# Set attention and gated feed-forward on one core: eight buffers for hi and lo, rows of x and transposed x in one ring

## Chip, cores and metric

One core of one Trainium2 chip runs the whole program. The metric is the device time in microseconds, the median of three runs; lower is better.

## What is computed

Input x has 4 batches of 12480 tokens with 128 channels. Each batch goes through two attentions with 32 inducing points, and every token of the result through a feed-forward layer with 2048 hidden units:

```python
h = mab(I, x)          # softmax(scale * I x^T) x: 32 rows per batch
a = mab(x, h)          # softmax(scale * x h^T) h: 12480 rows per batch
g = a @ w_in
g = g * (1 / (1 + exp(-1.702 * g)))
out = g @ w_out
```

The softmax of the first attention runs over all 12480 tokens of a batch, so the batch has to be read once for `h`, and a second time for the second attention.

## The kernel before, in words

**The feed-forward loop.** Tokens are worked in 98 items, 96 of 512 tokens and 2 of 384 (what is left over of two batches each). Each item has 8 steps, so there are 784 steps; a step is 256 of the 2048 hidden units. In a step PE makes two matrix products into a PSUM tile `ph` (L542, `firsts`). ACT turns `ph` into `g` with the gate function (L568). `g` is then split into a rounded part `hi`, by ACT straight from `ph` (L584) or by DVE from `g` (L591), and a rest `lo` = g - hi, by DVE (L600). Then PE makes six products into `pso`, three for each of two 128-row chunks: hi with the low part of the weights (L729), lo with the high part (L730), hi with the high part (L731). This is `seconds`. After 8 steps `pso` is copied out (L620 on ACT, L623 on DVE) and stored. The first 12 steps use whole weights instead (L715) and no hi and lo.

**The rings.** `ph` has 2 buffers, `g` 3, `hi` 6 and `lo` 6 (constant `HELD`). The tiles of hi and lo lie in a pool `ph_`; each has a gap of 16 elements behind it (`spaced`, `STEP`).

**The order of the work.** Nothing is scheduled on the chip: while the program is built, a planner (`Plan`) holds a list of threads, each a generator of jobs with an engine, an assumed duration, the buffers that they read, write and take, a rank and sometimes a gate. At each step it emits the job that can start first (start time plus its own delay, then rank). The order in which jobs are emitted is the fixed order of each engine's instructions, and of the DMAs in the queue of SP.

What steers it is the **lead**, `ahead()`: steps whose lo has been emitted (`counts["L"]`), less steps whose six products have been emitted (`counts["S"]/2`). `counts["F"]` is the number of steps whose first products have been emitted. The constants `AHEAD` = 4 and `LUMP` = 5 enter in four places:

- `late` (L507): first products are held back by 800 ns while the lead is at least `AHEAD`, and visits of the attention (groups of PE work, below) may then begin with a longer delay.
- `tarry` and `filler` (L510 to L514): attention work on ACT and DVE gets a delay of 400 ns and a low rank while the lead is below `AHEAD`.
- `by_then` (L516): the same, but only until `counts["F"]` has reached a due step.
- the exponentials (L907 and L1080): they need another table of ACT than the gate function, so they are put together in lumps of three or four sets. A lump may go when the lead is at least `LUMP`, or when `counts["F"]` has reached a last step.

**The attention of batches 1 to 3** runs beside the feed-forward loop, one batch ahead. For batch b (`attention`, L818): PE makes the first scores from transposed x (`first_into`, L352) in two or three visits; they are copied out and their maximum is taken; ACT makes two lumps of exponentials (L900); DVE transposes them; PE sums the rows of x with these weights in three visits (`weigh`, L371; `WEIGH` is [0, 1], [2, 3], [4, 5, 6]); a chain on DVE makes h; then `second` (L1032) makes the scores of the second attention from transposed x again (`second_into`, L360) in two visits, and two more lumps of exponentials (L1074). `lay_out` (L1110) normalizes them, splits them, and sends them by DMA into the tiles `st` that the first products read.

**The loads.** A batch is cut into seven sets: six of 2048 tokens and one of 192. Transposed x is loaded twice per batch, in 1 MB loads into the ring `r_xt` of 4 buffers (`loads_xT`, L744 to L761): all sets for the first scores, then all for the second. Rows of x are loaded once, in four DMAs of 256 KB for each set (`loads_x`, L763 to L777), into the ring `r_xn` of 2 buffers in the pool `pn`, which is opened when the last weights are decoded (`finish`, L1359); the loads wait for `counts["F"]` at 40 steps behind the batch's first (`loads_x` is spawned at L837). The two lists of loads are two threads of the planner; all go through the queue of SP.

Of the kernel before, what the change touches and what calls it, by code (L numbers as in the profile page):

```python
# [8 lines left out]
F32 = mybir.dt.float32  # L9
I32 = mybir.dt.int32  # L10
F32R = mybir.dt.float32r
# [6 lines left out]
P = 128  # L18
TOP = -(1 << 30)
TOK = 512  # L20
BLK = TOK // 32
RG = 2
HELD = 6
AHEAD = 4
LUMP = 5
LEAD = 24
SLACK = 3000.0
WC = 512
# [1 line left out]
XB = 4  # L30
# [66 lines left out]
class Ring:  # L97
# [8 lines left out]
    def free(self, ahead):  # L106
        k = len(self.units) + ahead - self.bufs
        if k < 0:
            return 0.0
        return self.units[k].gone if k < len(self.units) else None  # L110

    def take(self, unit):
        unit.ap = self.make()
        self.units.append(unit)


# [168 lines left out]
def set_attention_then_moe(ctx: ExitStack, tc, xT, x, indT, w_in, w_out, outT):  # L285
# [6 lines left out]
    NG = NCH // 2  # L292
    NTOT = xT.shape[1]
    B = 4
    N = NTOT // B
    SUP = G * TOK
    scale = 1.0 / math.sqrt(P)
    sups = []
# [5 lines left out]
    NS = len(sups)  # L304
# [3 lines left out]
    px = ctx.enter_context(tc.tile_pool(name="px", bufs=XB))  # L308
# [89 lines left out]
    first_block = {}  # L398
# [28 lines left out]
    plan = Plan()  # L427
# [5 lines left out]
    n = len(work) * NG  # L433
# [8 lines left out]
    x_units = {(0, s): Unit(4) for s in range(NS - 1)}  # L442
# [5 lines left out]
    x2_units = dict(x_units)  # L448
    x2_units[0, 1] = Unit(1)
    e_units = {(b, s): Unit(2, parts=4) for b in range(B) for s in range(NS)}  # L450
    hT_units = {0: Unit(99)}
    w_in_units = [Unit(999) for _ in range(G)]
    w_out_units = [Unit(9999, parts=2) for _ in range(G)]
# [3 lines left out]
    def spaced(pool, shape, tag, name):  # L457
        n_ = math.prod(shape[1:])

        def make():  # L460
            t = pool.tile([P, n_ + STEP], F32R, tag=tag, name=name)[:, 0:n_]
            return t.rearrange("p (c t) -> p c t", c=shape[1]) if len(shape) == 3 else t
        return make

    def of_pool(pool, shape, tag, name, dtype=F32, bufs=None):
        def make():
            return pool.tile(shape, dtype, tag=tag, name=name, bufs=bufs)
        return make

    r_xt = Ring(XB, of_pool(px, [P, SUP], "xt", "xt"))  # L470
# [30 lines left out]
    def ahead():  # L501
        return counts["L"] - counts["S"] / 2
# [4 lines left out]
    def late(least, most):  # L507
        return lambda: most if ahead() >= AHEAD else least

    def tarry():  # L510
        return 0.0 if ahead() >= AHEAD else 400.0

    def filler(rank=1):
        return lambda: (rank if ahead() >= AHEAD else 4, 0)  # L514

    def by_then(due):  # L516
        def rank():
            return (1 if ahead() >= AHEAD else 1.5 if counts["F"] >= due else 4, 0)

        def wait():  # L520
            return 0.0 if ahead() >= AHEAD or counts["F"] >= due else 400.0

# [218 lines left out]
    def since(i):  # L741
        return lambda: counts["F"] >= i

    def loads_xT():  # L744
        for b in range(1, B):
            for s in range(NS):
                x_units[b, s] = Unit(2 if s == NS - 1 else 1)
                x2_units[b, s] = x_units[b, s] if s == NS - 1 else Unit(1)
        some = [(0, x2_units, 1)]
        for b in range(1, B):  # L750
            some += [(b, x_units, s) for s in range(NS)]
            some += [(b, x2_units, s) for s in turn_of(b) if s < NS - 1]
        for b, units, s in some:
            t0, g, w = sups[s]
            u = units[b, s]
            ring = r_xl if s == NS - 1 else r_xt

            def emit(u=u, t0=t0, g=g, w=w):
                nc.sync.dma_start(u.ap[:, 0:g * w], xT[:, b * N + t0:b * N + t0 + g * w])

            yield Job("SP", emit, 430, 7600, takes=[(ring, u)], rank=(1, b), gate=lambda: loaded, size=g * w * 512)  # L761

    def loads_x(b, units, i0):  # L763
        for s in range(NS):
            t0, g, w = sups[s]
            u = units[s]
            for j in range(g):
                def emit(u=u, t0=t0, w=w, j=j):
                    r0 = b * N + t0 + j * w
                    nc.sync.dma_start(  # L770
                        u.ap[32 * j:32 * j + 32, 0:w // 32],
                        x[r0:r0 + w, :].rearrange("(k i) c -> i k c", i=32),
                    )
                yield Job(
                    "SP", emit, 430, 6800, takes=[(r_xnl if s == NS - 1 else r_xn, u)] if j == 0 else [], joins=[u] if j else [],
                    rank=(1, b), gate=lambda: "n" in pools and counts["F"] >= i0, size=2.4 * w * 512,
                )  # L777
# [5 lines left out]
    def turn_of(b):  # L783
        return list(range(NS)) if b % 2 == 0 else [NS - 1, *range(NS - 1)]
# [11 lines left out]
    class Bank:  # L796

        def __init__(self, unit, k=None):
            self.unit, self.k = unit, k
# [5 lines left out]
    def banks(n):  # L805
        if n <= 3:
            units = [Unit() for _ in range(n)]
            return [Bank(u) for u in units], [(r_pa if k < 2 else r_po, u) for k, u in enumerate(units)], None
        a, b, two = Unit(), Unit(), Unit(2)
        return [Bank(two, 0), Bank(two, 1), Bank(b), Bank(a)], [(r_pa, a), (r_pa, b), (r_ph, two)], r_ph  # L810
# [7 lines left out]
    def attention(b):  # L818

        i0 = first_block[b - 1, 0] * NG  # L820
# [12 lines left out]
            clear()  # L833
            cleared.at(plan.now + 200)
        yield Job("DVE", set_clear, 100, 200, rank=filler(), wait=tarry, gate=since(i0))
        xn = [Unit(parts=sups[s][1]) for s in range(NS)]
        plan.spawn(loads_x(b, xn, i0 + 40))  # L837
        s1 = [Unit(1) for _ in range(NS)]
        done = [Unit(9) for _ in range(NS)]

# [24 lines left out]
        for v, pair in enumerate(SCORE if b > 1 else WEIGH):  # L865
            pas, takes, first_in = banks(len(pair))
            room = kept(len(pair)) if first_in else inside if len(pair) > 2 else lambda: True

            def emit(pair=pair, pas=pas):
# [5 lines left out]
                takes, rank=(0, 0), gate=lambda v=v, room=room: counts["F"] >= i0 + 6 + (16 if b > 1 else 8) * v and room(),  # L875
# [17 lines left out]
        def first_exponentials(some):  # L893

            def emit():
# [10 lines left out]
                "ACT", emit, occ, occ + 150, [nmxu, cleared], [s1[s] for s in some], rank=(0, 0),  # L906
                gate=lambda: ahead() >= LUMP or counts["F"] >= i0 + 80, table="exp",  # L907
            )
# [22 lines left out]
        for v, some in enumerate(WEIGH):  # L931

            def emit(some=some, i=i):
# [8 lines left out]
                gate=since(i0 + 50 + 8 * v), slack=late(600, 2000),  # L942
# [89 lines left out]
    def second(b, visits, lumps, also=None):  # L1032
# [36 lines left out]
        def lump(some):  # L1069
            def emit():  # L1070
# [8 lines left out]
                "ACT", emit, occ, occ + 150, [ready[s] for s in some], [e_units[b, s] for s in some], rank=(0, 0),  # L1079
                gate=lambda: ahead() >= LUMP or counts["F"] >= last, table="exp", slack=lambda: 1500,  # L1080
            )
# [195 lines left out]
    def weights(k):  # L1277
# [78 lines left out]
        if inner or kept is not None:  # L1356
            finish()

    def finish():  # L1359
        decoded[0] += 1  # L1360
        if decoded[0] == 2 * G:
            late_.close()
            pools["n"] = ctx.enter_context(tc.tile_pool(name="pn", bufs=2, side="right"))

    wf = const.tile([P, WHOLE * WC], F32, name="wf") if WHOLE else None
    whf = wh.rearrange("p c d -> p (c d)")
# [1 line left out]
    loaded = []  # L1368
    raws = [Unit(6) for _ in range(2 * G)]
    decoded = [0, 0]  # L1370
    pools = {}
# [441 lines left out]
    def attentions():  # L1813
        yield from second(0, [([2, 3], since(10)), ([1, 4], since(10)), ([5, 6], since(10))], LUMPS)
        for b in range(1, B):
            yield from attention(b)
# [34 lines left out]
    plan.spawn(firsts())  # L1851
    plan.spawn(attentions())
    plan.spawn(loads_xT())
    plan.run(lambda: fasts[0] == 2 and fasts[3] == G and decoded[1] == SPLIT)
    plan.fill = None
# [3 lines left out]
    ph_ = ctx.enter_context(tc.tile_pool(name="ph_", bufs=HELD, reuse_waits="tile"))  # L1859
    po = ctx.enter_context(tc.tile_pool(name="po", bufs=2, reuse_waits="tile"))  # L1860
    r_g = Ring(3, of_pool(pg, [P, 2, TOK], "g", "g"))
    r_hi = Ring(HELD, spaced(ph_, [P, 2, TOK], "hi", "hi"))
    r_lo = Ring(HELD, spaced(ph_, [P, 2, TOK], "lo", "lo"))
    r_ob = Ring(2, of_pool(po, [P, TOK], "ob", "ob"))
    r_xn = Ring(2, lambda: pools["n"].tile([P, BLK, P], F32, tag="xn", name="xn"))
    r_xnl = Ring(1, lambda: pools["n"].tile([P, sups[-1][2] // 32, P], F32, tag="xn_last", name="xn_last", bufs=1))


# [36 lines left out]
```

## Time and profile before

| | |
|---|---|
| median of 3 runs | 1492.52 us (1492.43 to 1492.73) |
| the profiled execution's own time | 1495.18 us |
| its span, first to last instruction | 1493.3 us |
| mean granted clock of TensorE | 0.998 |
| busy: PE, DVE, ACT | 1474.7, 1334.4, 1315.0 us |
| busy share of the 16 DMA engines by queue 1 | 29.6% |

PE is one instruction behind the other nearly throughout, so what can be gained lies in the places where it stands or runs at a lower clock. Matmuls are pipelined: one takes some 380 ns from its first row to its last, while a new one starts some 216 ns after it (both from the rows below), so a short stand of PE can be hidden in its busy time.

### The profile page before, as it was taken

To read this page: it belongs to the slowest core of one execution; us is meant where nothing else is said; L and a number is where in the kernel's file an instruction comes from. 1 tells how busy PE (TensorE), PEld (TensorE's weight loads), DVE (VectorE), ACT (ScalarE), POOL (GpSimd) and SP (SyncE) were. 2 spreads that over 40 slices of the span, in tenths; PEclk is the share of its full clock that TensorE was granted. 3 is DMA by queue.
4 is the path that set the end of the run, shared out by engine and by line. 5 is a ranking of instruction groups with operands and counts; after the bars stand their busy time and mean duration, and the time that the engine had idled before them with its cause. 6 is when DMAs were issued, how large, how long until landed. Compare 5 with 4: busy or idle time off the path is not lost.

```text
span 1493.3 us, 21596 instructions
## 1 busy us (share of the span) xinstructions
PE 1474.7 (99%) x7707; PEld 1231.8 (82%) x7707; DVE 1334.4 (89%) x1647; ACT 1315.0 (88%) x1509; POOL 0.7 (0%) x6
## 2 busy tenths in 40 slices
PE   9999989999999999999999999999999999999999
PEld 7468878877888888887888888888878888888887
DVE  6999889898989998999899898999888998998987
ACT  6799898888989889988998999888988998898886
POOL 0000000000000000000000000000000000000000
PEclk9999999999999999999999999999999999999999
DMA  7366113434043514513414431540401111101100
GB/s 286 124 218 142 43 43 80 100 105 157 20 144 112 99 36 92 102 29 109 152 49 145 119 72 40 96 88 30 124 19 52 41 36 36 43 29 43 43 29 22
DMA packets 84873, 125.06 MB, mean 84 GB/s; under 512 B 12128, under 2 KB 52128, under 8 KB 79392
## 3 DMA queue, kind: packets, MB, share of 16 engines
q1 hardware_dynamic: 84768, 123.69, 29.6%
q8 instruction: 62, 1.02, 0.3%
q14 instruction: 43, 0.35, 0.1%
HBM read 70.43 MB, written 25.56 MB: 64 GB/s over the span
## 4 chain that ended last, share of the span: by engine, by line
PE 48%; ACT 2%; DVE 1%; issue 0%; ACTq 0%; DVEq 0%
PE ph L542 12%; PE pso L730 11%; PE pso L729 11%; PE pso L731 11%; ACT g L568 1%; DVE lo L600 1%; ACT hi L584 0%; DVE hi L591 0%; PE pa L371 0%; PE pa L352 0%; PE pso L645 0%; PE pso L643 0%; PE pso L644 0%; ACT e L900 0%; PE ph L360 0%
## 5 line engine op out<-in xcount | busy, mean ns | idle before, releaser
L600 DVE TENSOR_TENSOR lo<-g,hi 128x1024 fp32r<-128x1024 f32 (+1 forms) x772 | 923.1, 1214 | 107.7 <-ACT hi L584 98.6
L568 ACT ACTIVATE g<-ph 128x1024 f32<-128x1024 f32 (+1 forms) x784 | 812.8, 1045 | 142.0 <-PE ph L542 65.6
L730 PE MATMUL pso<-lo,wh 128*128 128x512 f32 (+1 forms) x1528 | 579.8, 379 | 1.6 <-DVE lo L600 1.4
L729 PE MATMUL pso<-hi,wl 128*128 128x512 f32 (+1 forms) x1528 | 580.0, 380 | 0.0
L731 PE MATMUL pso<-hi,wh 128*128 128x512 f32 (+1 forms) x1528 | 579.0, 379 | 0.0
L584 ACT ACTIVATE hi<-ph 128x1024 fp32r<-128x1024 f32 (+1 forms) x471 | 494.8, 1053 | 0.6 <-PE pso L731 0.5
L542 PE MATMUL ph<-st,hw 128*128 128x512 f32 x1536 | 452.0, 387 | 10.7 <-ACT g L568 6.6
L542 PEld LDWEIGHTS ph<-st,hw 128*128 128x128 f32 x1536 | 281.5, 190 | 80.1 <-ACT g L568 16.9
L730 PEld LDWEIGHTS pso<-lo,wh 128*128 128x128 f32 x1528 | 289.8, 190 | 44.7 <-DVE lo L600 4.1
L729 PEld LDWEIGHTS pso<-hi,wl 128*128 128x128 f32 x1528 | 290.0, 190 | 40.1 <-issue 0.2
L731 PEld LDWEIGHTS pso<-hi,wh 128*128 128x128 f32 x1528 | 290.0, 190 | 39.5
L591 DVE CAST hi<-g 128x1024 fp32r<-128x1024 f32 (+1 forms) x301 | 202.8, 682 | 18.5 <-ACT g L568 18.0
L620 ACT COPY ob<-pso 128x512 f32<-128x512 f32 (+1 forms) x64 | 39.2, 613 | 5.9 <-PE pso L731 5.7
L623 DVE COPY ob<-pso 128x512 f32<-128x512 f32 x33 | 22.7, 688 | 5.6 <-PE pso L731 5.2
L715 PE MATMUL pso<-g,wf 128*128 128x512 f32 x48 | 23.1, 597 | 0.1
L352 PE MATMUL pa<-xt,indT_sb 128*32 128x512 f32 x160 | 19.9, 598 | 0.0
L371 PEld LDWEIGHTS pa<-xn,t 128*32 128x32 f32 x576 | 15.2, 110 | 3.0 <-issue 2.6
L371 PE MATMUL pa<-xn,t 128*32 128x128 f32 x576 | 17.6, 274 | 0.0
L1158 DVE TENSOR_TENSOR t<-t,two 128x512 f32<-128x512 f32 (+1 forms) x27 | 16.7, 619 | 0.2 <-ACT two L1147 0.2
L1142 DVE STREAM_TRANSPOSE t<-e 128x512 f32<-128x512 f32 x23 | 16.2, 705 | 0.1
L1137 DVE TENSOR_TENSOR e<-e,sm 128x512 f32<-128x512 f32 x23 | 15.7, 681 | 0.0
L1064 DVE TENSOR_TENSOR e<-e,m 128x512 f32<-128x512 f32 x23 | 15.6, 682 | 0.0
(204 smaller groups left out, 478.6 us busy)
## 6 DMA issues: line engine op xcount, KB each, us to landing
xt<-in_xT SPq DMA_DIRECT2D x42, 1024.0 KB, 7.1
out_T<-ob SPq DMA_DIRECT2D x95, 256.0 KB, 2.0
xn<-in_x SPq DMA_DIRECT2D x72, 256.0 KB, 6.2
st<-two SPq DMA_DIRECT2D x184, 64.0 KB, 2.0
st<-t SPq DMA_DIRECT2D x184, 64.0 KB, 2.0
hw<-t SPq DMA_DIRECT2D x48, 64.0 KB, 2.0
raw<-in_w_in SPq DMA_DIRECT2D x4, 512.0 KB, 9.4
raw<-in_w_out SPq DMA_DIRECT2D x4, 512.0 KB, 5.2
```

Source lines behind the costliest of these rows:

```text
L371: pe_.matmul(pa[32 * j:32 * j + 32, 0:P], aT[0:q, kk, :], xn[0:q, kk] if second is None or kk < BLK // 2 else second[0:q, kk - BLK // 2], ...
L542: pe_.matmul(ph[:, c, at:at + w], u.ap[:, ch % 4 * P:(ch % 4 + 1) * P], order(st[:, at:at + w]), start=True, stop=True,)
L568: act.activation(gs[i].ap[:, :, 0:w], phs[i].ap[:, :, 0:w], AF.Gelu_apprx_sigmoid)
L584: act.activation(his[i].ap[:, :, 0:w], phs[i].ap[:, :, 0:w], AF.Gelu_apprx_sigmoid)
L591: dve.tensor_copy(his[i].ap[:, :, 0:w], gs[i].ap[:, :, 0:w])
L600: dve.tensor_sub(los[i].ap[:, :, 0:w], gs[i].ap[:, :, 0:w], his[i].ap[:, :, 0:w].bitcast(F32))
L620: act.copy(runs(ob.ap[:, 0:w], bi), unwoven(pso.ap[:, 0:w], bi))
L623: dve.tensor_copy(runs(ob.ap[:, 0:w], bi), unwoven(pso.ap[:, 0:w], bi))
L715: pe_.matmul(pso.ap[:, 0:w], wf[:, ch * P:(ch + 1) * P], gs[i].ap[:, c, 0:w], start=(ch == 0), stop=(ch == NCH - 1),)
L729: pe_.matmul(o, wl[:, ch, :], hi, start=(ch == 0), stop=False)
L730: pe_.matmul(o, wh[:, ch, :], lo, start=False, stop=False)
L731: pe_.matmul(o, wh[:, ch, :], hi, start=False, stop=(ch == NCH - 1))
```

## The change

`HELD` stays 6 for the pool `ph_`, and two more buffers for hi and two for lo (`MORE`) are taken from the pool `pn` once it is open; `Grown` puts them into the ring. They have no gap of 16 elements. `AHEAD` goes from 4 to 6, `LUMP` from 5 to 6. To make room, rows of x lose their 2 buffers in `pn` and use the 4 buffers of `r_xt`, with one common list of units. `loads_xT` now yields all loads of a batch in one list: transposed x for the first scores, rows of x, transposed x for the second attention. The step count at which rows of x may be loaded is the same as before.

```diff
-AHEAD = 4
-LUMP = 5
+MORE = 2
+AHEAD = 6
+LUMP = 6
...
+class Grown(Ring):
+    def __init__(self, bufs, make, more, makes):
+        super().__init__(bufs, make)
+        self.more, self.makes, self.since = more, makes, None
+
+    def look(self):
+        if self.since is None and self.makes():
+            self.since, self.first = len(self.units), self.make
+            self.bufs += self.more
+
+    def free(self, ahead):
+        self.look()
+        return super().free(ahead)
+
+    def take(self, unit):
+        self.look()
+        k = None if self.since is None else (len(self.units) - self.since) % self.bufs
+        unit.ap = self.makes()() if k is not None and k < self.more else self.make()
+        self.units.append(unit)
...
-        some = [(0, x2_units, 1)]
-        for b in range(1, B):
-            some += [(b, x_units, s) for s in range(NS)]
-            some += [(b, x2_units, s) for s in turn_of(b) if s < NS - 1]
-        for b, units, s in some:
+        def load(b, units, s):
...
-            yield Job("SP", emit, 430, 7600, takes=[(ring, u)], rank=(1, b), gate=lambda: loaded, size=g * w * 512)
+            return Job("SP", emit, 430, 7600, takes=[(ring, u)], rank=(1, b), gate=lambda: loaded, size=g * w * 512)
+
+        yield load(0, x2_units, 1)
+        for b in range(1, B):
+            for s in range(NS):
+                yield load(b, x_units, s)
+            yield from loads_x(b, first_block[b - 1, 0] * NG + 40)
+            for s in turn_of(b):
+                if s < NS - 1:
+                    yield load(b, x2_units, s)
...
-        xn = [Unit(parts=sups[s][1]) for s in range(NS)]
-        plan.spawn(loads_x(b, xn, i0 + 40))
+        xn = xn_units[b]
...
-            pools["n"] = ctx.enter_context(tc.tile_pool(name="pn", bufs=2, side="right"))
+            pools["n"] = ctx.enter_context(tc.tile_pool(name="pn", bufs=1, side="right"))
...
-    r_hi = Ring(HELD, spaced(ph_, [P, 2, TOK], "hi", "hi"))
-    r_lo = Ring(HELD, spaced(ph_, [P, 2, TOK], "lo", "lo"))
+    def grown(name):
+        def make():
+            return pools["n"].tile([P, 2, TOK], F32R, tag=name, name=name, bufs=MORE)
+
+        return Grown(HELD, spaced(ph_, [P, 2, TOK], name, name), MORE, lambda: "n" in pools and make)
+
+    r_hi, r_lo = grown("hi"), grown("lo")
...
-    r_xn = Ring(2, lambda: pools["n"].tile([P, BLK, P], F32, tag="xn", name="xn"))
+    r_xn = Ring(XB, lambda: px.tile([P, SUP], F32, tag="xt", name="xn").rearrange("p (k c) -> p k c", c=P))
+    r_xn.units = r_xt.units
```

## Rows read from the trace of the kernel before

**Rows 1.** The page: span, part 1 (busy time and instructions by engine)

```profile
span 1493.3 us, 21596 instructions
...
PE 1474.7 (99%) x7707; PEld 1231.8 (82%) x7707; DVE 1334.4 (89%) x1647; ACT 1315.0 (88%) x1509; POOL 0.7 (0%) x6
```

**Rows 2.** The page, part 5: line, engine, operation, count, busy us, mean ns, idle before

```profile
L600 DVE TENSOR_TENSOR lo<-g,hi 128x1024 fp32r<-128x1024 f32 (+1 forms) x772 | 923.1, 1214 | 107.7 <-ACT hi L584 98.6
...
L731 PE MATMUL pso<-hi,wh 128*128 128x512 f32 (+1 forms) x1528 | 579.0, 379 | 0.0
...
L1158 DVE TENSOR_TENSOR t<-t,two 128x512 f32<-128x512 f32 (+1 forms) x27 | 16.7, 619 | 0.2 <-ACT two L1147 0.2
```

**Rows 3.** Waits of PE from 100 to 1463 us: total us, times, longest

```profile
PE ph L542 <- ACT g L568: 6.6, 13, 3.2
PE ph L542 <- ACT hi L584: 3.7, 4, 1.7
PE pso L730 <- DVE lo L600: 1.1, 3, 0.7
```

**Rows 4.** Windows: start:end, length, PE, PEld, DVE, ACT, POOL busy (instructions), clock, DMA, GB/s

```profile
211.00:225.00 14.00, 10.41 (x92) 7.92 (x93) 9.19 (x12) 12.26 (x22) 0.00 (x0) 0.88 0.23 59
357.00:370.00 13.00, 11.53 (x43) 8.66 (x41) 8.53 (x10) 10.20 (x14) 0.00 (x0) 0.87 0.10 23
439.00:452.00 13.00, 13.00 (x67) 10.29 (x60) 12.12 (x18) 12.94 (x16) 0.00 (x0) 1.00 0.81 327
924.80:940.00 15.20, 13.64 (x118) 11.05 (x116) 11.04 (x15) 13.75 (x25) 0.00 (x0) 1.00 0.72 130
1080.00:1095.00 15.00, 12.87 (x58) 10.00 (x56) 9.89 (x13) 11.23 (x13) 0.00 (x0) 1.00 0.12 35
1163.00:1463.00 300.00, 300.00 (x1389) 261.53 (x1388) 273.03 (x290) 269.54 (x295) 0.00 (x0) 1.00 0.13 37
100.00:1463.00 1363.00, 1351.31 (x6907) 1148.37 (x6906) 1232.37 (x1451) 1218.89 (x1377) 0.00 (x0) 1.00 0.28 75
870.00:924.85 54.85, 54.85 (x255) 47.69 (x254) 51.72 (x65) 51.59 (x59) 0.00 (x0) 1.00 0.14 39
```

**Rows 5.** Windows of L600 alone, up to the start of three table loads

```profile
0.00:211.00 211.00, 86.53 (x72) 1.00 0.46 149
0.00:439.36 439.36, 228.92 (x193) 0.99 0.39 116
0.00:1079.97 1079.97, 643.09 (x538) 1.00 0.37 102
```

**Rows 6.** Windows of L730 alone, the same stretches

```profile
0.00:211.00 211.00, 54.30 (x142) 26.87 (x142) 1.00 0.46 149
0.00:439.36 439.36, 143.28 (x376) 71.63 (x376) 0.99 0.39 116
0.00:1079.97 1079.97, 406.66 (x1070) 203.22 (x1071) 1.00 0.37 102
```

**Rows 7.** Timeline of ACT around 211 us: start, length, instruction

```profile
211.00 1.28 ACT L900 ACT_TABLE_LOAD   x1
212.29 0.73 ACT L900 ACTIVATE e<-e,nmx 128x512 f32<-128x512 f32 x1
...
217.01 1.28 ACT L568 ACT_TABLE_LOAD   x1
```

**Rows 8.** Line L371 (weighted sums) on PE, 254 to 335 us

```profile
L371 PE MATMUL pa<-xn,t x128: 272/273/297, 258.8 to 298.9; 128*32 128x128 f32 x128
```

**Rows 9.** Line L360 (second scores) on PE, 254 to 335 us

```profile
L360 PE MATMUL ph<-xt,hTb x24: 592/593/617, 316.1 to 330.9; 128*32 128x512 f32 x24
```

**Rows 10.** The page, part 6: DMA issues, KB each, median us to landing

```profile
xt<-in_xT SPq DMA_DIRECT2D x42, 1024.0 KB, 7.1
```

**Rows 11.** Tile left (sets of 192 tokens), 360 to 450 us: first and last start

```profile
L542 PE MATMUL ph<-left,hw x32: 245/275/321, 416.2 to 427.1; 128*128 128x192 f32 x32
...
L1175 SPq DMA_DIRECT2D left<-t x8: 507/585/1700, 391.6 to 403.8; - x8
```

More of the change, by code (lines that the diff above doesn't have):

```diff
@@ L450, in set_attention_then_moe @@
     e_units = {(b, s): Unit(2, parts=4) for b in range(B) for s in range(NS)}
+    xn_units = {b: [Unit(parts=sups[s][1]) for s in range(NS)] for b in range(1, B)}
     hT_units = {0: Unit(99)}
@@ L759, in emit, with loads_x @@
                 nc.sync.dma_start(u.ap[:, 0:g * w], xT[:, b * N + t0:b * N + t0 + g * w])
-            yield Job("SP", emit, 430, 7600, takes=[(ring, u)], rank=(1, b), gate=lambda: loaded, size=g * w * 512)
-    def loads_x(b, units, i0):
+            return Job("SP", emit, 430, 7600, takes=[(ring, u)], rank=(1, b), gate=lambda: loaded, size=g * w * 512)
[7 more added lines that the diff above has]
+                    yield load(b, x2_units, s)
+    def loads_x(b, i0):
         for s in range(NS):
             t0, g, w = sups[s]
-            u = units[s]
+            u = xn_units[b][s]
             for j in range(g):
```

## The prediction

> **What bounds the kernel now.** I read the page's busy times first: PE is busy 1474.7 of 1493.3 us, DVE and ACT 89% and 88% [rows 1]. So a gain can only come from places where PE stands, and from the clock. The waits of PE between start and end say where that is [rows 3]: 17 of its 20 waits are first products (L542) that wait for ACT to empty a `ph` buffer, 3 are products that wait for lo, and none is for a DMA. The windows show when. From 1163 to 1463 us PE is busy 300.00 of 300.00 us [rows 4]; 1389 matmuls start there, one every 0.216 us, so a step of eight takes 1.73 us. The larger stands lie at lumps of exponentials: PE is idle 3.59 us in the window from 211 us, 1.47 from 357, 1.56 from 924.8, 2.13 from 1080, and 11.69 us in the whole stretch from 100 to 1463 us [rows 4], so 2.94 us in smaller places.
>
> A lump takes ACT away from the gate function: the one at 211 us runs from the first table load to the end of the second, 217.01 + 1.28 - 211.00 = 7.29 us [rows 7]. Meanwhile PE lives on finished steps. I take the lead from counts: lo instructions begun (L600) less half of the L730 matmuls begun up to the start of the lump [rows 5, 6]. It is 72 - 142/2 = 1 step at 211 us, 538 - 535 = 3 at 1080 us, and 193 - 188 = 5 at 439 us, and there, with 5, PE doesn't stand at all [rows 4]. One step of lead is worth six products, 6 x 0.216 = 1.30 us. So the shortage is of lead at the lumps, and 4 is where the planner begins to hold first products back.
>
> **What is at stake.** Idle time, 11.7 us. The clock: the granted clock is 0.88 over 14 us and 0.87 over 13 us [rows 4], between the two levels 1.2 and 2.4 GHz, in both cases where PE had just stood; that is 0.12 x 14 + 0.13 x 13 = 3.4 us of work not done. And what hides in busy time: a matmul is booked for 0.379 us [rows 2] but blocks the next for only 0.216, so each of the 20 waits costs some 0.16 us more than the idle time shown, 3.3 us. Together 18.4 us, the most that can be won.
>
> **The change part by part.**
>
> *Two more buffers, AHEAD 6.* Nothing is added to any engine: the same products, gate functions, splits. First products are now held back from a lead of 6 on instead of 4, and attention work on ACT and DVE goes first only from 6 on. Two steps more of lead before a lump are 2.6 us of cover. To build them ACT and DVE must run ahead once per lump: 269.54 and 273.03 us for 1389/8 = 174 steps [rows 4] are 1.55 and 1.57 us a step, so 3.1 us each for two steps. Before the lump at 924.85 us the 55 us stretch has 3.26 and 3.13 us of idle time on them [rows 4], just that and nothing to spare. Over the whole stretch ACT is idle 144 us and DVE 131 [rows 4], so elsewhere there is room. Hence: the stands at 357 and 1080 us and the small ones, all under 2.6 us, go, 1.47 + 2.13 + 2.94 = 6.5; with the stand at 357 goes its clock loss, 1.7; the one at 924.8 loses half, 0.8; the one at 211 loses 2.6 of 3.59, and I let its clock loss stay. 15 of 20 waits take their hidden 0.16 us along, 2.4. Sum 14.0 us.
>
> *LUMP 6.* Lumps wait for a lead of 6 or their last step. Six steps are 7.8 us of cover, more than the longest lump. But the two lumps of first exponentials, seven sets behind one table load at 211 us, may now be parted, since the second finds a lower lead. That is one pair of loads more for each of three batches, 3 x 2 x 1.28 us [rows 7] = 7.7 us of ACT. Its cost on PE lies between nothing (ACT's 144 idle us hide it) and all 7.7 us; I take 1.5, near the lower end, because a lump that goes by its lead has its cover. If that cover is gone, each pair takes 2.57/1.55 = 1.7 steps of lead. The Trainium skill, "ScalarE: Activation LUTs", section "What ACT_TABLE_LOAD costs", tells to batch by table: about 1283 ns a load and about 1380 ns of drain for every switch. The trace agrees on the load and shows no drain: the first exponential starts at 212.29, right behind it. By the page the extra switches would be 16 us of ACT, and my share of them 3 us, so 1481.5 us.
>
> *The tiles themselves.* The new ones lie in `pn`, without the gap of 16 elements. No row shows hi or lo without it. Nearest is L1158, which reads and writes tiles without a gap: 619 ns for 512 columns against 1214 for 1024 in L600 [rows 2], the same rate, so nothing on DVE. For PE's reads the lower bound is zero and the upper one open; 5% on the products of two in eight steps would be 190 x 6 x 0.011 = 12.5 us. I take zero, by the DVE row. Before the first use they wait for the last reader of the decoded weights' space; at most one lo, 1.2 us [rows 2], and I take zero.
>
> *The loads.* The number of DMAs is the same. Rows of x move into the ring of transposed x and pass ahead of the loads for the second scores, which so start later. A buffer of sets 4 and 5 of batch 1 is read until 298.9 us [rows 8]; the second scores begin at 316.1 us and need sets 0 and 1, whose buffers the visit at 258.8 frees; the last ones begin at 330.9 [rows 8, 9]. A load lands in 7.1 us [rows 10]. So 17 us or more cover 7.1; nothing lost. If a load were late, PE would stand for it in the visit, with every first product behind: up to 7.1 us at each of six visits, 43 us, the upper end. A gain is excluded, as PE waits for no DMA now [rows 3]. What can be held up behind them in SP's queue are the DMAs into `st`; those for the left-over sets were issued up to 403.8 and first read at 416.2 [rows 11], 12 us of cover. Zero.
>
> **Sum.** 14.0 - 1.5 = 12.5 us. On the profiled execution: span 1493.3 to 1480.8, its own time 1495.2 to 1482.7. That execution lay 2.7 us above the median of 1492.5; against the median I get 1480.0 us. What is late next is the lump at 211 us, and then nothing but PE's own 1.73 us a step.
>
> **The rivals.**
>
> *Lead doesn't come.* Not AHEAD but the work on ACT and DVE sets the lead before a lump. For it: the lead of 1 at 211 us and 3 at 1080 [rows 5, 6], below the old 4 already. Against: at 439 it was 5, and idle time is there. Then the stands at 211, 357 and 924.8 stay, and 2.13 + 2.94 us and ten waits, 1.6 us, go, less 1.5 to 3 for table loads: about 4.5 us, 1488.
>
> *Nothing changes.* Lumps go at their last step as before and find the lead they found; or the extra loads eat what is won. 1492.
>
> *Attention comes late (slower).* Work on DVE and ACT for batch 1 waits 400 ns a job until the lead is 6, which it reaches later than 4. Before, its second lump fell in the window from 357 us [rows 4], the DMAs into the left-over tile were issued from 391.6 to 403.8 and PE first read it at 416.2 [rows 11]. So the chain may slip by 391.6 - 357 = 35 us, less some 5 for the lump itself (an estimate, a part of the 7.29 us of seven sets [rows 7]), and 12 us from the last DMA to the read, 42 us or 24 steps. From there on PE stands a microsecond for each. A slip of 54 us, half of the stretch from 100 to 211 us, costs 12 us at this place, and with 4.5 won elsewhere gives 1500. For it: DVE idles only 11% of the time. Against: due steps force most of this work.
>
> *Tiles without a gap (slower).* 12.5 us lost on PE's reads eat 12.5 won and anything beyond makes it slower; with the lead of the first rival, 1500.
>
> **How the numbers follow.** Forecast 0.62, own range 1475 to 1487: from nearly all of the 18.4 us to half of the sum, 7.0 less 1.5 for the table loads. Lead doesn't come 0.16; nothing changes 0.08; attention late 0.10; tiles 0.04. A measurement of this kernel tells 0.2% from no change, 3 us, so under 1489.5 is faster and over 1495.5 slower. Faster is 0.62 and 0.10 of the first rival's 0.16, 0.72; the same 0.06 + 0.08 = 0.14; slower 0.14. The range goes from the most that can be won, 1474, to 1493, which takes in the first two rivals and leaves out the slower ones, 0.14, and a few hundredths of the tails.
>
> **What would show it.** Right: from 100 to 1463 us the idle time of PE falls from 11.7 to about 4 us; no window at a lump but the first has a clock under 1.00; counts of L600 and L730 show a lead of 5 or 6 at most lumps; six more table loads on ACT. Wrong: the lead at lumps is 3 or less as before (first rival); first products wait for a DMA into `st` or left, or visits for xt or xn (attention or loads); the spacing in a quiet stretch is over 0.216 us (tiles).

## The result, and the profile after

1479.51 us median of 4 runs (1478.92 to 1479.92), before 1492.51 (1492.43 to 1492.73): 13.0 us less, ratio 0.9912 with a 95% interval of 0.9895 to 0.993. Faster, and 0.5 us from the 1480.0 us forecast.

The page of the changed kernel: span, busy times, and the groups that answer to [rows 1] and [rows 2] (line, engine, operation, count, busy us, mean ns, idle before). Lines have moved: L542 is now L567, L568 L593, L584 L609, L600 L625, L729 to L731 L754 to L756, L360 L384, L371 L395, L900 L929, L1074 L1103.

```profile
span 1477.1 us, 21560 instructions
...
PE 1469.1 (99%) x7707; PEld 1226.4 (83%) x7707; DVE 1336.5 (90%) x1649; ACT 1314.9 (89%) x1507; POOL 0.7 (0%) x6
...
L625 DVE TENSOR_TENSOR lo<-g,hi 128x1024 fp32r<-128x1024 f32 (+1 forms) x772 | 922.0, 1214 | 98.9 <-ACT hi L609 88.5
...
L756 PE MATMUL pso<-hi,wh 128*128 128x512 f32 (+1 forms) x1528 | 577.5, 378 | 0.0
```

The work is nearly the same: PE's 7707 matmuls, 772 times lo at 1214 ns each and the 1528 matmuls of L756 as of L731 before; DVE has two instructions more and ACT two fewer. The span fell by 16.2 us. Where it came from shows in the waits of PE from 100 to 1463 us (total us, times, longest), against [rows 3]:

```profile
PE ph L567 <- ACT g L593: 0.8, 4, 0.2
PE pa L1047 <- DVE hTb L1009: 0.2, 1, 0.2
PE ph L567 <- ACT hi L609: 0.2, 1, 0.2
```

Six waits instead of 20, 1.2 us instead of 11.4, the longest 0.2 instead of 3.2. The windows at the same five lumps, one quiet stretch and the whole, against [rows 4] (start:end, length, PE, PEld, DVE, ACT, POOL busy, clock, DMA share, GB/s):

```profile
218.90:233.00 14.10, 13.87 (x119) 11.56 (x118) 9.53 (x12) 12.26 (x23) 0.00 (x0) 1.00 0.21 60
363.90:377.00 13.10, 13.10 (x61) 10.97 (x60) 11.32 (x25) 13.07 (x17) 0.00 (x0) 1.00 0.90 346
461.80:475.00 13.20, 13.20 (x63) 11.56 (x62) 10.72 (x15) 10.76 (x13) 0.00 (x0) 1.00 0.09 20
911.10:926.40 15.30, 15.09 (x124) 12.53 (x123) 10.62 (x14) 13.45 (x24) 0.00 (x0) 1.00 0.69 138
1064.10:1079.10 15.00, 15.00 (x70) 12.75 (x69) 12.12 (x15) 13.28 (x17) 0.00 (x0) 1.00 0.17 54
1163.00:1450.00 287.00, 287.00 (x1329) 249.54 (x1328) 260.68 (x275) 257.32 (x281) 0.00 (x0) 1.00 0.13 37
100.00:1463.00 1363.00, 1361.65 (x6979) 1156.78 (x6978) 1250.37 (x1468) 1235.64 (x1393) 0.00 (x0) 1.00 0.29 76
```

PE is idle 0.23 us at the first lump where it was 3.59, 0.21 at the fourth where it was 1.56, and not at all at the other three. The granted clock is 1.00 everywhere; it had been 0.88 and 0.87 in two windows. Over the whole stretch idle time went from 11.69 to 1.35 us. The spacing of matmuls in the quiet stretch is 287.00/1329 = 0.216 us as before.

The lead at the start of the lumps, by the counting of [rows 5, 6]. First L625 (lo) alone, then L755 (products with lo) alone, each up to the start of three table loads:

```profile
0.00:218.96 218.96, 96.16 (x81) 1.00 0.46 135
0.00:461.82 461.82, 249.79 (x210) 1.00 0.40 117
0.00:1064.14 1064.14, 642.32 (x538) 1.00 0.37 103
```

```profile
0.00:218.96 218.96, 57.17 (x150) 28.49 (x151) 1.00 0.46 135
0.00:461.82 461.82, 154.87 (x410) 77.49 (x410) 1.00 0.40 117
0.00:1064.14 1064.14, 403.36 (x1066) 201.46 (x1066) 1.00 0.37 103
```

81 - 150/2 = 6 steps at the first lump, where it was 1; 210 - 205 = 5; 538 - 533 = 5, where it was 3.

The span adds up: idle time 10.3 us from 100 to 1463 us, clock 3.4, and 14 waits fewer at the 0.16 us that each hides in busy time (an estimate from the matmul's 0.379 and 0.216 us), 2.3, make 16.0 of 16.2 us. The last two agree with the page: PE's busy time fell by 1474.7 - 1469.1 = 5.6 us. The medians differ by 13.0 only: the 42 executions of the kernel before in this study lie at 1492.2 to 1493.0 us or at 1494.2 to 1495.6 us, with a little more clock lost in the longer ones (mean 0.997 to 0.998 against 0.998 to 0.999), and the profiled one, 1495.18, is like these. The changed kernel ran at 1.000 each time.

### The profile page after: what moved, and what is told of

Same layout as the page of the kernel before. It is cut to its first block, busy times and chain, and to the rows that moved or that the text cites. A ratio compares the mean times of both kernels' runs of the same rounds, so it can differ in the third digit from the quotient of the medians.

```text
span 1477.1 us, 21560 instructions
## 1 busy us (share of the span) xinstructions
PE 1469.1 (99%) x7707; PEld 1226.4 (83%) x7707; DVE 1336.5 (90%) x1649; ACT 1314.9 (89%) x1507; POOL 0.7 (0%) x6
## 4 chain that ended last, share of the span: by engine, by line
PE 88%; ACT 6%; DVE 4%; issue 1%; SPq 0%; DMA 0%; POOLq 0%; ACTq 0%; POOL 0%; DVEq 0%
PE ph L567 22%; PE pso L755 20%; PE pso L754 20%; PE pso L756 20%; ACT g L593 2%; ACT hi L609 1%; DVE lo L625 1%; PE pa L376 1%; PE pa L395 1%; PE pa L384 1%; ACT e L929 1%; PE ph L384 1%; PE pso L740 1%; SPq L1204 0%; PE pso L1849 0%
## 5 line engine op out<-in xcount | busy, mean ns | idle before, releaser
L625 DVE TENSOR_TENSOR lo<-g,hi 128x1024 fp32r<-128x1024 f32 (+1 forms) x772 | 922.0, 1214 | 98.9 <-ACT hi L609 88.5
L593 ACT ACTIVATE g<-ph 128x1024 f32<-128x1024 f32 (+1 forms) x784 | 812.8, 1046 | 129.1 <-PE ph L567 63.5
L754 PE MATMUL pso<-hi,wl 128*128 128x512 f32 (+1 forms) x1528 | 578.5, 379 | 0.0
L755 PE MATMUL pso<-lo,wh 128*128 128x512 f32 (+1 forms) x1528 | 577.9, 378 | 0.4 <-DVE lo L625 0.3
L756 PE MATMUL pso<-hi,wh 128*128 128x512 f32 (+1 forms) x1528 | 577.5, 378 | 0.0
L609 ACT ACTIVATE hi<-ph 128x1024 fp32r<-128x1024 f32 x475 | 498.8, 1050 | 0.8 <-PE pso L756 0.7
L567 PE MATMUL ph<-st,hw 128*128 128x512 f32 x1536 | 453.7, 385 | 1.2 <-ACT g L593 0.8
L567 PEld LDWEIGHTS ph<-st,hw 128*128 128x128 f32 x1536 | 279.1, 189 | 69.9 <-ACT hi L609 14.8
L755 PEld LDWEIGHTS pso<-lo,wh 128*128 128x128 f32 x1528 | 288.8, 189 | 42.5 <-DVE lo L625 1.8
L754 PEld LDWEIGHTS pso<-hi,wl 128*128 128x128 f32 x1528 | 288.8, 189 | 40.6 <-issue 0.2
L756 PEld LDWEIGHTS pso<-hi,wh 128*128 128x128 f32 x1528 | 288.8, 189 | 40.0
L395 PEld LDWEIGHTS pa<-xn,t 128*32 128x32 f32 x576 | 15.2, 110 | 3.0 <-issue 2.7
L395 PE MATMUL pa<-xn,t 128*32 128x128 f32 x576 | 17.6, 274 | 0.0
L1171 DVE STREAM_TRANSPOSE t<-e 128x512 f32<-128x512 f32 x23 | 16.2, 704 | 0.0
```

The lines of the kernel that those rows point to most:

```text
L395: pe_.matmul(pa[32 * j:32 * j + 32, 0:P], aT[0:q, kk, :], xn[0:q, kk] if second is None or kk < BLK // 2 else second[0:q, kk - BLK // 2], ...
L567: pe_.matmul(ph[:, c, at:at + w], u.ap[:, ch % 4 * P:(ch % 4 + 1) * P], order(st[:, at:at + w]), start=True, stop=True,)
L593: act.activation(gs[i].ap[:, :, 0:w], phs[i].ap[:, :, 0:w], AF.Gelu_apprx_sigmoid)
L609: act.activation(his[i].ap[:, :, 0:w], phs[i].ap[:, :, 0:w], AF.Gelu_apprx_sigmoid)
L625: dve.tensor_sub(los[i].ap[:, :, 0:w], gs[i].ap[:, :, 0:w], his[i].ap[:, :, 0:w].bitcast(F32))
L754: pe_.matmul(o, wl[:, ch, :], hi, start=(ch == 0), stop=False)
```

## The experiments

Twelve kernels, each compared with runs of the kernel before on the same chip. That kernel's median beside them was 1494.4, 1494.2 or 1492.8 us, after 1492.5 beside the change, so the ratios carry the comparison with it. The changed kernel and its near variants spread by a microsecond or so, and their times are compared directly, though they ran on different chips.

**The buffers alone.** Everything of the change but the two targets:

```diff
-AHEAD = 6
-LUMP = 6
+AHEAD = 4
+LUMP = 5
```

> Eight buffers and the one list of loads, but AHEAD 4 and LUMP 5 as before. Theory (PE stands because the planner holds the lead at 4, and the buffers matter only as room for a longer lead): leads at the lumps stay at 1 to 5, PE keeps about 11 us of idle time, time 1489.5 to 1494. Rival (a deeper ring by itself smooths the flow of hi and lo): at least half of the 13 us, 1480 to 1486.

1498.63 us, ratio 1.0031 (1.002 to 1.0043): slower than six buffers. The rival falls. The theory holds in its direction, a deeper ring is nothing by itself, but it had no loss in it, and the time is 4.6 us above its range. Counts of L625 and of L755 up to two of the lumps, and windows at these lumps and over the whole:

```profile
0.00:570.04 570.04, 317.30 (x266) 1.00 0.39 109
0.00:1081.71 1081.71, 644.75 (x538) 1.00 0.37 102
```

```profile
0.00:570.04 570.04, 200.58 (x529) 100.26 (x529) 1.00 0.39 109
0.00:1081.71 1081.71, 406.79 (x1072) 203.01 (x1072) 1.00 0.37 102
```

```profile
570.00:585.00 15.00, 12.42 (x104) 9.66 (x103) 10.84 (x15) 13.22 (x24) 0.00 (x0) 0.89 0.82 146
1081.70:1096.00 14.30, 11.72 (x46) 9.34 (x45) 7.73 (x10) 10.40 (x14) 0.00 (x0) 0.88 0.11 30
100.00:1463.00 1363.00, 1349.22 (x6890) 1143.75 (x6889) 1230.30 (x1446) 1217.73 (x1374) 0.00 (x0) 1.00 0.29 76
```

The lead is 266 - 529/2 = 1.5 at 570 us, where the kernel before had 265 - 262 = 3, and 538 - 536 = 2 at 1081.7 us, where it had 3. PE is idle 2.6 us at both and the clock is 0.89 and 0.88. In the kernel before, the second lump of batch 1 went at 439 us by its lead of 5; here it went at 537.94 us, and the next lump came 32 us later, before the lead had been made up. The lump at 924.47 us is alike: the one ahead of it came at 901.60 us, where it had been at 847.24, and its lead is 456 - 907/2 = 2.5, where it had been 4. For the lower lead at 1081.7 us the runs show no cause.

**The targets alone.** The kernel before with the two constants of the change:

```diff
-AHEAD = 4
-LUMP = 5
+AHEAD = 6
+LUMP = 6
```

> The kernel before with AHEAD 6 and LUMP 6: six buffers, loads as before. Theory (a lead of 6 needs more than six buffers, since the step that PE reads holds one too): the lead at the lumps stops at about 4 to 5, part of the stands remain, 1483 to 1488. Rival A (the two targets alone do it, six buffers are enough): 1478.5 to 1481. Rival B (a target that is never reached only makes attention work wait): over 1492.

1489.53 us, ratio 0.9973 (0.9962 to 0.9984). Faster, 1.5 us above the range given; rivals A and B fall. The lead at the three lumps of first exponentials is 84 - 161/2 = 3.5, 265 - 525/2 = 2.5 and 457 - 454 = 3, below the 4 to 5 of the theory and the 6, 5.5 and 5.5 of the changed kernel by the same counts. Idle time over the stretch is half gone:

```profile
100.00:1463.00 1363.00, 1356.66 (x6933) 1143.86 (x6932) 1239.35 (x1459) 1225.56 (x1379) 0.00 (x0) 1.00 0.28 75
```

6.3 us, after 11.7 before and 1.35 with both parts. Neither half of the change does it: buffers without targets 0.3% slower, targets without buffers 0.3% faster, together 0.9% faster.

**Seven buffers.** The changed kernel with

```diff
-MORE = 2
+MORE = 1
```

> The changed kernel with one more buffer of hi and lo instead of two, seven in all; AHEAD 6 and LUMP 6. Six buffers with these targets measured 1489.5, eight 1479.5. Theory (each buffer is a step of lead, 1.3 us of cover at each lump): between them, 1481 to 1487. Rival (there is a sill: a lead of 6 is reached with seven already): 1478.5 to 1481.

1486.38 us, ratio 0.9949 (0.9934 to 0.9964), PE idle 5.5 us:

```profile
100.00:1463.00 1363.00, 1357.46 (x6947) 1147.04 (x6947) 1241.62 (x1464) 1228.68 (x1386) 0.00 (x0) 1.00 0.29 76
```

Between six (1489.5, with the old loads) and eight (1479.5), as the theory has it. By the times the seventh buffer wins 3 us and the eighth 7, by the ratios 3.6 and 5.5, so it isn't certain that the steps differ. Idle time goes from 6.3 to 5.5 and 1.35 us; where the rest of the seventh's 3 us lies is not shown.

**The loads alone.** The one list of loads and the shared ring, nothing else:

```diff
-MORE = 2
-AHEAD = 6
-LUMP = 6
+MORE = 0
+AHEAD = 4
+LUMP = 5
```

> Only the one list of loads and the shared ring of four; six buffers of hi and lo, AHEAD 4 and LUMP 5. Theory (the loads cost nothing and win nothing, PE waits for no DMA before or after): 1491 to 1494, no wait of PE for xt or xn. Rival (the later loads for the second scores make a visit wait, 7 us each): over 1495; or they ease the DMA queue: under 1489.5.

1494.72 us beside 1494.4, ratio 0.9999 (0.9989 to 1.0008). That is 0.7 us above the theory's range, which was laid around 1492.5, while the kernel before had 1494.4 here. The waits of PE are close to those of [rows 3], with one short wait for lo fewer and another of 0.2 us more, and none is for a DMA:

```profile
PE ph L567 <- ACT g L593: 6.6, 13, 3.2
PE ph L567 <- ACT hi L609: 3.7, 4, 1.6
PE pso L755 <- DVE lo L625: 0.9, 2, 0.7
PE ph L567 <- DVE e L1080: 0.2, 1, 0.2
```

The loads cost nothing and win nothing; they make room.

**No gaps at all.** All eight buffers of hi and lo without the 16 elements:

```diff
-        return Grown(HELD, spaced(ph_, [P, 2, TOK], name, name), MORE, ...)
+        return Grown(HELD, of_pool(ph_, [P, 2, TOK], name, name, F32R), MORE, ...)
```

> The changed kernel with the gap of 16 elements taken from the six other buffers of hi and lo too, so that none of the eight has it. Theory (the gap is worth nothing on DVE or PE at this place, so the two new tiles without it cost nothing): within 2 us of the changed kernel, 1478 to 1481.5, matmuls in the quiet stretch still 0.216 us apart. Rival (PE or DVE read tiles without a gap more slowly): three times the cost that the change already carries, over 1483.

1479.2 us, ratio 0.9901 (0.9886 to 0.9916). Idle time and spacing are those of the changed kernel:

```profile
100.00:1463.00 1363.00, 1361.65 (x6978) 1156.75 (x6978) 1250.17 (x1468) 1235.85 (x1393) 0.00 (x0) 1.00 0.29 76
1163.00:1450.00 287.00, 287.00 (x1329) 249.56 (x1328) 260.69 (x275) 257.33 (x281) 0.00 (x0) 1.00 0.13 37
```

So the missing gap of the two new tiles costs nothing here, which no row of the trace before could show for PE's reads.

**Lumps parted.** The two lumps of first exponentials of a batch kept six steps apart:

```diff
-                gate=lambda: ahead() >= LUMP or counts["F"] >= i0 + 80, table="exp",
+                gate=lambda: (ahead() >= LUMP or counts["F"] >= i0 + 80) and (
+                    some[0] == 0 or fired and counts["F"] >= fired[0] + 6), table="exp",
```

(`fired` takes `counts["F"]` when a lump is emitted.)

> The changed kernel with the two lumps of first exponentials of each batch kept six steps apart, so three more pairs of table loads of 1.28 us each, 7.7 us of ACT. Theory (ACT has idle time and each lump has its lead): between nothing and 1.5 us lost, 1479 to 1481.5; or even won, as each half is shorter. Rival (ACT is as good as full, its time comes out on PE): 1484 to 1488.

1481.53 us, ratio 0.9913 (0.9899 to 0.9928). Lines L929 of the changed kernel and L930 here, table loads of the first exponentials among those of the other lines:

```profile
L593 ACT ACT_TABLE_LOAD x7 | 9.0, 1283 | 0.1
L609 ACT ACT_TABLE_LOAD x5 | 6.4, 1283 | 0.0
...
L929 ACT ACT_TABLE_LOAD x3 | 3.8, 1283 | 0.0
```

```profile
L930 ACT ACT_TABLE_LOAD x6 | 7.7, 1283 | 0.1
```

Six loads instead of three; with the way back six loads more, 7.7 us of ACT. By the times the kernel is 2 us longer, a quarter of that; by the ratios nothing can be told. PE doesn't stand for it at the parted lumps: its largest idle time in this run, 1.70 us, lies behind another lump, at 348.8 us. The time is at the upper end of the theory's 1479 to 1481.5; the rival falls. Here the measurement also bears on the page "ScalarE: Activation LUTs" of the Trainium skill, section "What ACT_TABLE_LOAD costs": its 1283 ns a load is the mean of these rows. By its further 1380 ns of drain the six would be 16 us of ACT, an estimate from the page; no run shows that drain, and in each of these rows ACT is idle 0.1 us or less before all its loads together.

**Longer lumps.** A direct measure of what covers a lump: 12 activations more in each lump of first exponentials, on a tile of ones that keeps its value.

```diff
             def emit():
+                for _ in range(12):
+                    act.activation(ones, ones, AF.Exp, scale=0.0)
                 for s in some:
```

> The changed kernel with 12 more small activations of 128 columns (on a constant, whose values stay as they are) in each of the two lumps of first exponentials of batches 1 to 3: some 2.2 us more of ACT per lump, 4.4 us for the two together, 13 us in all. Theory (at these lumps PE lives on the lead, of which 0.5 to 1 step, 0.7 to 1.3 us, was left after them in the changed kernel): what goes beyond comes out as a stand of PE, 3 to 4 us at each of three places, 1487 to 1492 with some clock loss. Rival (ACT's idle time in the stretch takes it up, as the lead is not what covers a lump): under 1483.

1501.34 us, ratio 1.0051 (1.0036 to 1.0066). Longer than expected, because the additions were: the timeline of ACT at the first of these lumps, and the first wait of PE behind it (start, length, instruction, idle before):

```profile
219.05 1.28 ACT L926 ACT_TABLE_LOAD   x1
220.34 4.06 ACT L926 ACTIVATE ones<-ones 128x128 f32<-128x128 f32 x12
...
227.13 4.05 ACT L926 ACTIVATE ones<-ones 128x128 f32<-128x128 f32 x12
```

```profile
235.32 2.14 PE L567 MATMUL ph<-st,hw 128*128 128x512 f32 x4 [6.61 <-ACT hi L609]
```

```profile
219.00:237.00 18.00, 11.39 (x105) 9.38 (x104) 5.58 (x7) 16.87 (x44) 0.00 (x0) 0.85 0.55 101
```

Twelve take 4.06 us, not 2.2; perhaps because each works on the tile of the one before, which no run tests. The two lumps together are 8.1 us longer. The lead at their start is 6 by the same counts, as in the changed kernel, and PE stands 6.61 us. So 1.5 us of the 8.1 were still covered, about the one step that the theory took to be left. At the second place, 565.8 us, PE stands 7.16 us. At the third the two lumps went apart, at 902.15 and 933.42 us, and the longest stand there is 1.31 us. It is the lead that covers a lump, and where the two go together most of what is beyond it is time of PE, with the lower clock on top (0.85 in the window shown).

**Other targets on eight buffers.** Five more settings:

```diff
 AHEAD, LUMP of the changed kernel: 6, 6
+LUMP = 5                # e6_lump_5
+LUMP = 4                # e10_lump_4
+AHEAD = 7; LUMP = 5     # e12_ahead_7
+AHEAD = 8; LUMP = 8     # e7_ahead_8
+AHEAD = 4; LUMP = 4     # e9_old_ahead_lump_4
```

> The changed kernel with LUMP back at 5, AHEAD 6. Theory (what pays is the lead that AHEAD lets grow; a lump that goes at 5 has 6.5 us of cover, little less than the longest lump): 1478 to 1483. Rival (the gain is in the lumps' own threshold, which keeps them from going too early): 1485 to 1490.

> The changed kernel with LUMP 4, AHEAD 6. LUMP 6 measured 1479.5, LUMP 5 1478.4. Theory (PE stands hardly any more, so there is nothing left to win; a lump at 4 has 5.2 us of cover, less than the 7.3 us of the two lumps together but more than one of them): 1477.5 to 1482. Rival (leads of 4 are used up by the lumps and the stands come back): over 1484.

> The changed kernel with AHEAD 7 and LUMP 5. AHEAD 6 with LUMP 5 measured 1478.4, AHEAD 8 with LUMP 8 1483.2. Theory (with lumps that go in time a longer target costs little; PE stands about 1 us in all): 1477.5 to 1481. Rival (what was lost with 8 and 8 came from AHEAD, attention work that waits too long): 1482 to 1485.

> The changed kernel with AHEAD 8 and LUMP 8, which eight buffers can hardly reach. Theory (attention work then waits for its due steps and lumps go at their last step, while the lead at them is 5 to 6 all the same): 1478 to 1486, with lumps later than in the changed kernel. Rival (the slower case of the forecast: the chain of the attention comes so late that first products wait for st, left or hw): over 1492.

> Eight buffers with AHEAD 4 and LUMP 4. With AHEAD 4 and LUMP 5 they measured 1498.6, slower than six. Theory (those lumps waited for a lead that AHEAD 4 kept just out of reach, and then fell together at their last steps; with LUMP 4 they go in time, each with 4 steps, 5.2 us of cover): 1487 to 1494. Rival (the eight buffers themselves are what hurts at a short lead): 1496 to 1500.

| AHEAD, LUMP | us | ratio (95%) |
|---|---|---|
| 6, 5 | 1478.41 | 0.9896 (0.9879 to 0.9912) |
| 6, 6, the change | 1479.51 | 0.9912 (0.9895 to 0.993) |
| 6, 4 | 1480.16 | 0.9909 (0.9895 to 0.9924) |
| 7, 5 | 1479.91 | 0.9909 (0.9894 to 0.9924) |
| 8, 8 | 1483.19 | 0.9928 (0.9913 to 0.9943) |
| 4, 4 | 1495.13 | 1.0004 (0.9995 to 1.0014) |
| 4, 5, buffers alone | 1498.63 | 1.0031 (1.002 to 1.0043) |

The first four settings lie in the ranges of their theories, and their rivals fall. Around the change the time is flat: with 6, 5 PE is idle 0.98 us, and a microsecond is all that could still differ. It has the lowest time of all, 1478.16 to 1478.78 in four runs; on the same chip the kernel without gaps had 1478.62 to 1479.64, so that it beats the change is not shown.

```profile
100.00:1463.00 1363.00, 1362.02 (x6982) 1156.49 (x6981) 1249.30 (x1473) 1236.62 (x1392) 0.00 (x0) 1.00 0.29 76
```

With 8, 8 the time is in the theory's range and the attention is not late, but the lead at the lumps is not 5 to 6 throughout. Lumps go later, one of them at 184.56 us, 27 us ahead of the next at 211.50, and there one stand of 1.9 us comes back. The wait in question, and the counts of L625 and of L755 up to the start of these two lumps:

```profile
PE ph L567 <- ACT g L593: 1.9, 1, 1.9
```

```profile
0.00:184.56 184.56, 73.30 (x62) 1.00 0.51 153
0.00:211.50 211.50, 88.58 (x74) 1.00 0.47 138
```

```profile
0.00:184.56 184.56, 42.41 (x111) 20.97 (x111) 1.00 0.51 153
0.00:211.50 211.50, 54.87 (x144) 27.20 (x144) 1.00 0.47 138
```

The lead is 62 - 111/2 = 6.5 at the first and 74 - 144/2 = 2 at the second.

With 4, 4 the loss against six buffers is gone but nothing is won; the time is 1.1 us above the range of the theory and 0.9 below that of its rival. That the lumps' threshold made the buffers slower at 4, 5 agrees with this. Between 4, 4 and 6, 4 AHEAD alone differs, 1495.13 against 1480.16 us: the gain hangs on AHEAD, with the buffers.

## Why the prediction was right

**What bounds the kernel.** Right. The stands of PE at the lumps and the clock behind them were what could be won: idle time, clock and the estimate of what hides in busy time make 16.0 of the 16.2 us of span.

**Two steps more of lead.** Right in kind, and too small at two places. At the lump of 1080 us the lead grew from 3 to 5 as assumed, and the stand went. At the one of 211 us it was to grow by two and leave 1 us of idle time and the low clock; it grew from 1 to 6, and 0.23 us and no clock loss are left. The step assumed that each lump keeps what it had and gets two more. But the lead of 1 came after the lump at 188 us, 23 us earlier. Counts of L600 and of L730 in the kernel before, up to its start:

```profile
0.00:188.37 188.37, 74.61 (x62) 1.00 0.50 161
```

```profile
0.00:188.37 188.37, 44.71 (x117) 22.14 (x117) 1.00 0.50 161
```

There it had been 62 - 117/2 = 3.5. In the changed kernel this lump went already at 152.16 us, at a lead of 43 - 74/2 = 6, and there were 67 us to make it up before 218.96. With 8, 8 the two lumps were again 27 us apart, and in spite of the eight buffers the lead fell to 2. So the distance between lumps has a part in it that the prediction left out; no run changed the distance alone. At 924.8 us half was to stay, because the idle time before it seemed to be just enough; 0.21 us stayed.

**LUMP 6 and table loads.** The charge of 1.5 us for six more loads was wrong: the table loads are 26 as before, and the first lumps of a batch still go together. Parting them by force costs 2 us by the times.

**The sum.** 14.0 - 1.5 us was too low for the execution on which it was made, 12.5 against 15.3 in its own time and 16.2 in its span. It met the median, 13.0, because the median of the kernel before holds less of the clock loss than its profiled execution; I took the whole 2.7 us between the two as an offset that stays. That the forecast lies within 0.5 us is therefore in part two errors that cancel.

**Tiles and loads at zero.** Right, both measured: 1479.2 without any gap, ratio 0.9999 for the loads alone.

**The rivals.** "Lead doesn't come" falls with the counts above. "Attention comes late" went the other way. The tile of the left-over sets, against [rows 11]:

```profile
L567 PE MATMUL ph<-left,hw x32: 246/275/350, 407.3 to 418.1; 128*128 128x192 f32 x32
...
L1204 SPq DMA_DIRECT2D left<-t x8: 508/563/589, 367.9 to 382.5; - x8
```

Its DMAs were issued from 367.9 to 382.5 us, 21 to 24 us earlier than before, and the first read came at 407.3, so they had 25 us of cover instead of 12. Lumps that go by their lead don't wait for their last step, so the attention came early. Even with a target of 8 the case did not come.

## What to carry to other kernels

Where the bound engine only stands while a helper is away for a known time, measure the lead of finished work at that moment, in steps, and multiply by the work per step: that is the cover, and what is missing is the loss, within a step or two. Count in the steps that other engines still finish while the helper is away (below). A ring and the scheduler's target for it are one change; here buffers without the target lost 0.3%, the target without buffers won 0.3%, and both won 0.9%. Ask of each such moment also how long ago the last one was: at the worst place the lead grew by five steps, not two, when the one before came 67 us ahead instead of 23.

## What was not expected

- A stand of PE need not cost clock: the trace with seven buffers has waits up to 2.4 us at a clock of 1.00 throughout, and that with eight and targets of 4 and 5 has stands of the same 2.4 us with clocks of 0.87 to 0.89, beside one of 2.3 us at 924.5 us with a clock of 1.00. What decides it is not shown.
- The lead by itself doesn't give the size of a stand to better than a step or two: in the kernel before, 4 steps at 924.85 us left 1.56 us of idle time, 3 at 570.44 only 0.5, though both lumps take 7.3 us. The trace of DVE shows a step that the count misses. DVE made two more lo after the lump at 570.44 us had begun, from `g` that was there already; at 924.85 us the last one had begun just ahead of the lump, and the next came after it:

```profile
570.75 1.22 DVE L600 TENSOR_TENSOR lo<-g,hi 128x1024 fp32r<-128x1024 f32 x1
...
572.61 1.22 DVE L600 TENSOR_TENSOR lo<-g,hi 128x1024 fp32r<-128x1024 f32 x1
```

```profile
924.78 1.18 DVE L600 TENSOR_TENSOR lo<-g,hi 128x1024 fp32r<-128x1024 f32 x1
...
933.20 1.23 DVE L600 TENSOR_TENSOR lo<-g,hi 128x1024 fp32r<-128x1024 f32 x1 [4.09 <-ACT hi L584]
```

So PE had 3 + 2 = 5 steps to live on there and 4 here, a difference of one step, 1.30 us, beside 1.1 us in the idle time.
